# Retention attention feeding a leaky two-layer network: three more units transposed on TensorE, three more loaded through GpSimd's ring, zero matmuls in the opening, and layer-one blocks reordered

## The chip, the cores and the metric

The kernel runs on one core of one Trainium2 chip. A core has five engines that work at the same time and meet through semaphores: TensorE (PE in the profile: matmuls, and PEld its weight loads), VectorE (DVE), ScalarE (ACT), GpSimd (POOL) and SyncE (SP). SP, ACT and POOL also issue DMAs. The metric is the device time of one execution in microseconds (us); lower is better.

## The reference

```python
# q, k, v: batch 8, heads 8, sequence 576, head size 64 (float32)
scores = (q @ k^T) / 8
ret    = scores * Dmat         # Dmat[h, i, j] = gamma_h ** (i - j) for i >= j, else 0
x      = (ret @ v), heads side by side      # 4608 tokens x 512
h      = x @ w_in                           # 512 -> 2048
out    = max(0.01 * h, h) @ w_out           # 2048 -> 512, float32
```

There is no softmax, so the product with the decay can be done in chunks of 64 rows, with a running state (k^T v, 64x64 for each head) that carries what came before.

## The kernel before, in words

**Units.** Each batch's 576 rows are cut into four units of 128 rows and one of 64, 40 units in all. Units 4, 9, 14 and so on are the half ones. For a unit, `load` brings its q, k and v from HBM into tiles `t32` (one DMA each; six buffers for each of q, k and v). `cast_qk` writes 16-bit k (on ACT, L138) and q times a decay table (L139, on DVE for units under 8, on POOL from 8 on) into `qk16`; `cast_v` (L159) does the same for v. Both q and k are needed with the head dimension on the partitions, in `qkT`. For units under `NPE = 4` `transposes` does this on TensorE (eight 128x128 matmuls against an identity, L177, into the PSUM tile `yps`, copied out by ACT and DVE, L182). For all others `cast_qk` issues a transposing DMA from SP (L147).

**Attention of a unit.** `scores` (L194, L204) makes the chunk products and the state products in the PSUM tile `sc`, of which there is one buffer; `masks` (L214) and `states` (L228 to L242) read it on DVE, and ACT or POOL cast the state `st`. `outputs` (L296, L306; `outputs_acc`, L262 and L273, for the first four units) makes the unit's columns of `xT`, the 16-bit transposed input of the network: PE into `ot`, ACT copies (L314), DVE adds (L320).

**Network.** Tokens are cut into groups: three of 256, seven of 512, one of 256. A block of layer one (`g1_blocks`, L413) is eight matmuls of 256 columns or four of 512, followed by the leaky activation on ACT (L420) into `gt`. A block of layer two (`g2_blocks`, L436) is four matmuls of 512 columns; after sixteen of them DVE copies the result (L446) and SP stores it. `blocks(g, part, ...)` runs two blocks of layer one of group g for each part, sixteen matmuls. The layer two of groups 0 and 1 is done by `g2_wide` (L481): sixteen pieces of four matmuls, called in portions by `some(a, b)`, with four results in PSUM at once; DVE copies them (L490) and SP stores them (L492).

**Order.** The schedule is by hand: each engine runs its instructions in the order in which the program makes them. Lines 502 to 569 write out the opening, units 0 to 6 woven with groups 0 and 1. Units from 7 on are `steady(n)` steps: loads of unit n+4 (SP), scores of n, outputs of n-1, masks and states of n, casts of n+2 and with them its transposing DMA. `run` threads these steps between blocks of the network; the first such call holds the steps of units 7 to 11 among sixteen blocks of group 2.

**Loads.** Unit 0's k goes through SP. The rest of units 0 to 8, `w_in` (sixteen DMAs) and `w_out` (four) are issued by POOL and lie in one ring. Units 9 and 10 are issued by SP after the last piece of `g2_wide`, and units from 11 on by the steps. The transposing DMAs and the stores of results share SP's ring with SP's loads.

Of the kernel before, what the change touches and what calls it, by code (L numbers as in the profile page):

```python
# [9 lines left out]
FP = mybir.dt.float32  # L10
F16 = mybir.dt.float16
# [6 lines left out]
def kernel(  # L18
# [22 lines left out]
    nc = tc.nc  # L41
# [3 lines left out]
    P = 128  # L45
    CH = 64
    BLK = 256
    NP = H // 2
    NF = DFF // P
    TOK = 512  # L50
# [20 lines left out]
    const_pool = ctx.enter_context(tc.tile_pool(name="const", bufs=1))  # L71
# [4 lines left out]
    sc_pool = ctx.enter_context(tc.tile_pool(name="scp", bufs=1, space=PSUM))  # L76
    ot_pool = ctx.enter_context(tc.tile_pool(name="otp", bufs=1, space=PSUM))
    h_pool = ctx.enter_context(tc.tile_pool(name="hpp", bufs=2, space=PSUM))
    y_pool = ctx.enter_context(tc.tile_pool(name="yp", bufs=2, space=PSUM))
# [4 lines left out]
    ident = const_pool.tile([P, P], F16, name="ident")  # L84
# [11 lines left out]
    units = [(b, w) for b in range(B) for w in range((S + P - 1) // P)]  # L96
    NU = len(units)
    nrows = [min(P, S - P * w) for b, w in units]
    NPE = 4
    NFIRST = 7  # L100
    NEARLY = 8
    t32 = {}
    qk16 = {}
    v16 = {}
    qkT = {}
# [10 lines left out]
    def load(u, x, eng):  # L116
        b, w = units[u]
        n = nrows[u]
        t = ld_pool.tile([P, H, D], FP, name=f"t32_{x}")
        t32[u, x] = t  # L120
        eng.dma_start(  # L121
            out=t[0:n],
            in_=(q, k, v)[x][b, :, P * w : P * w + n, :].rearrange("h t d -> t h d"),
        )

    def loads(u, eng):
        for x in (1, 0, 2):
            load(u, x, eng)

    def cast_qk(u):  # L130

        if u >= NU:
# [5 lines left out]
        nc.scalar.copy(out=t[0:n, 1], in_=t32[u, 1][0:n])  # L138
        (nc.vector if u < NEARLY else nc.gpsimd).tensor_tensor(  # L139
            out=t[0:n, 0],  # L140
# [3 lines left out]
        )  # L144
        if u >= NPE:
            qkT[u] = a_pool.tile([P, 2, NP, P], F16, name="qkT")
# [5 lines left out]
    def cast_v(u):  # L152
        if u >= NU:
# [4 lines left out]
        v16[u] = t  # L158
        (nc.vector if u < NEARLY else nc.gpsimd).tensor_tensor(  # L159
            out=t[0:n],  # L160
# [5 lines left out]
    def casts(u):  # L166
        cast_qk(u)
        cast_v(u)

    def transposes(u):  # L170

        n = nrows[u]
        qkT[u] = a_pool.tile([P, 2, NP, P], F16, name="qkT")
        for x in (1, 0):
            tr = y_pool.tile([P, NP, P], F16, name="yps")
            for p in range(NP):
                nc.tensor.transpose(  # L177
                    tr[:, p, :],
                    qk16[u][:, x, 2 * p : 2 * p + 2, :].rearrange("t h d -> t (h d)"),
                    ident,  # L180
                )
            (nc.scalar.copy if x else nc.vector.tensor_copy)(out=qkT[u][:, x], in_=tr)  # L182

    sc_tiles = {}

    def scores(u):

        nb = nrows[u] // CH
        a = sc_pool.tile([P, 2, 2, NP, CH], FP, name="sc")
        sc_tiles[u] = a  # L190
        for p in range(NP):
            for g in range(2):
                for j in range(nb):
                    nc.tensor.matmul(  # L194
                        out=a[half(j), g, 0, p, :],
                        lhsT=qkT[u][half(g), 1, p, half(j)],
                        rhs=qkT[u][half(g), 0, p, half(j)],
                        start=True, stop=True, skip_group_check=True,
                    )
        if nb == 2:  # L200
            for p in range(NP):
                for j in range(2):
                    for g in range(2):
                        nc.tensor.matmul(  # L204
                            out=a[half(g), j, 1, p, :],
                            lhsT=qk16[u][half(j), 1, 2 * p + g, :],
                            rhs=v16[u][half(j), 2 * p + g, :],
                            start=True, stop=True, skip_group_check=True,
                        )

    def masks(u):
        n = nrows[u]
        s16s[u] = a_pool.tile([P, 2, NP, CH], F16, name="s16")
        nc.vector.tensor_tensor(  # L214
            out=s16s[u][0:n],
            in0=sc_tiles[u][0:n, :, 0],
            in1=mask_sb[0:n].unsqueeze(1).unsqueeze(1).to_broadcast([n, 2, NP, CH]),
            op=MUL,
        )

    def states(u):
        b, w = units[u]
        if nrows[u] < P:
            return
        st = sc_tiles[u][:, :, 1]
        s32 = a_pool.tile([P, 2, NP, CH], FP, name="s32")
        if w == 0:
            nc.vector.tensor_copy(out=s32[:, 0], in_=st[:, 0])  # L228
        else:
            nc.vector.tensor_tensor(out=s32[:, 0], in0=st[:, 0], in1=carry[b], op=ADD)  # L230
        if w % 2 == 0:
            nc.vector.tensor_tensor(out=s32[:, 1], in0=st[:, 1], in1=s32[:, 0], op=ADD)  # L232
        else:
            tmp = a_pool.tile([P, NP, CH], FP, name="stmp")
            nc.vector.tensor_tensor(out=tmp, in0=st[:, 1], in1=s32[:, 0], op=ADD)
            nc.vector.tensor_tensor(
                out=s32[:, 1], in0=tmp,
                in1=gblk_sb.unsqueeze(2).to_broadcast([P, NP, CH]), op=MUL,
            )
        carry[b] = s32[:, 1]  # L240
        st16[u] = a_pool.tile([P, 2, NP, CH], F16, name="st16")
        (nc.scalar.copy if u < NEARLY else nc.gpsimd.tensor_copy)(out=st16[u], in_=s32)  # L242

# [5 lines left out]
    def outputs_acc(u):  # L249

        n = nrows[u]
        b, w = units[u]
        ot = ot_pool.tile([P, 2, 2 * NP, CH], FP, name="ot")
        o_all = ot[:, 0].rearrange("q (p j) t -> q p j t", j=2)
        seen = set()
        for r in range(2):
            if r:
                nc.tensor.drain()
            for p in range(NP):
                for hh in range(2):  # L260
                    o = hh ^ swap(p)
                    nc.tensor.matmul(  # L262
                        out=o_all[half(o), p, r, :],
                        lhsT=v16[u][half(r), 2 * p + hh, :],
                        rhs=s16s[u][half(r), hh, p, :],
                        start=o not in seen, stop=False, skip_group_check=True,
                    )
                    seen.add(o)
            for j in range(2):
                if w == 0 and j == 0:  # L270
                    continue
                for p in (0, 2, 1, 3):
                    nc.tensor.matmul(  # L273
                        out=o_all[half(r ^ swap(p)), p, j, :],
                        lhsT=st_before(u, j)[half(r), p, :],
                        rhs=qkT[u][half(r), 0, p, half(j)],
                        start=False, stop=True, skip_group_check=True,
                    )
        t0 = (b * S + P * w) % XR
        nc.scalar.copy(  # L280
            out=xT[:, :, t0 : t0 + n], in_=o_all.rearrange("q p j t -> q p (j t)")
        )
# [62 lines left out]
    nc.vector.memset(warm, 0.0)  # L345
    nc.scalar.activation(out=warm, in_=warm, func=mybir.ActivationFunctionType.Lrelu)
    nc.vector.memset(zst, 0.0)

    load(0, 1, nc.sync)
    load(0, 0, nc.gpsimd)  # L350
# [10 lines left out]

    def steady(n):
        def go():
            if n + 4 < NU:
                loads(n + 4, nc.sync)
            if n < NU:
                scores(n)
            if n > NFIRST:
                outputs(n - 1)
            if n < NU:  # L370
                masks(n)
                states(n)
            casts(n + 2)

        steps.append((n - 1, go))
# [120 lines left out]
    def blocks(g, *parts):  # L496
        for fq in parts:
            for m in (2 * fq, 2 * fq + 1):
                g1[g][m]()
# [5 lines left out]
    cast_v(1)  # L505
    transposes(1)
    scores(0)
    masks(0)
    cast_qk(2)
    states(0)  # L510
    cast_v(2)
    for u in (2, 3):
        transposes(u)
        scores(u - 1)
        outputs_acc(u - 2)
        masks(u - 1)
        if u == 2:
            cast_qk(3)
        states(u - 1)
        if u == 2:  # L520
            cast_v(3)
# [4 lines left out]
    states(3)  # L526
    blocks(0, 1)
    outputs_acc(3)
    blocks(1, 0, 1)
    blocks(0, 2)  # L530
    blocks(1, 2)
    for u in (5, 6):
        loads(u, nc.gpsimd)
        load_w_out(u - 4)
    load_w_out(3)
    for u in (7, 8):
        loads(u, nc.gpsimd)
    casts(4)
    blocks(0, 3)
    casts(5)  # L540
    blocks(1, 3)

    wide = g2_wide([(0, 0), (0, 1), (1, 0), (1, 1)])
# [1 line left out]
    def some(a, b):  # L545
        for m in range(a, b):
            wide[m]()

    some(0, 3)
    scores(4)  # L550
    masks(4)
    some(3, 6)
    scores(5)
    outputs(4)
    masks(5)
    states(5)
    casts(6)
    some(6, 11)
    scores(6)
    outputs(5)  # L560
    masks(6)
    states(6)
    some(11, 13)
    outputs(6)
    some(13, 16)
    loads(9, nc.sync)
    casts(7)
    loads(10, nc.sync)
    casts(8)
    run(ends[3], g1[2] + g2_blocks(2))  # L570
    run(ends[4], g1_blocks(3))
# [33 lines left out]
```

## Time and profile before

| | |
|---|---|
| time, median of 3 runs | 352.72 us (351.57 to 354.4) |
| the profiled execution: its own time / its span | 352.5 us / 350.7 us |
| PE busy | 301.6 us, 86% of the span |
| DVE, ACT, POOL busy | 144.3, 134.4, 114.7 us |
| HBM read, written | 36.78 MB, 9.44 MB |
| POOL's ring (q0), SP's ring (q1) | 10.62 MB in 6400 packets, 39.73 MB in 126112 packets |

The span runs from the first to the last instruction; the execution's own time is 1.8 us more. In the page's slices each digit is the busy share of a fortieth of the span (8.77 us) in tenths. A timeline row reads: start, duration, engine, line, operation, output<-inputs, shapes, count; in brackets how long the engine stood idle just before and what released it. Rows of one kind that follow each other are merged and counted.

### The profile page before, as it was taken

Reading aid. Unit: us, or ns where it says so; the run is one execution under the profiler, and the core shown is the slowest. Engines: PE = TensorE matmul, PEld = TensorE weight load, DVE = VectorE, ACT = ScalarE, POOL = GpSimd, SP = SyncE. Lnnn points to the kernel's source line nnn. Section 1 sums busy time; section 2 is a strip of 40 time slices with the busy share of each in tenths; the row PEclk is TensorE's granted clock in tenths of the full one; section 3 lists DMA queues with packets and bytes.
Section 4 is the critical chain, followed back from the end, with each engine's and each line's share of the span. In section 5 each row is a group of like instructions: output and inputs, shape, how many; then the busy total and the mean of one; then the engine's idle time right before and its main releaser. Section 6 shows DMA issues by size and latency. Waiting matters only on the chain.

```text
span 350.7 us, 8376 instructions
## 1 busy us (share of the span) xinstructions
PE 301.6 (86%) x3544; PEld 155.8 (44%) x3544; DVE 144.3 (41%) x322; ACT 134.4 (38%) x237; POOL 114.7 (33%) x139
## 2 busy tenths in 40 slices
PE   1589955844849559999999999999999999999995
PEld 0367722323624224444444444444444444445552
DVE  2741202471536654633446256435634653200111
ACT  3345600132513456443454445445444534332220
POOL 8787612002442445252235043522252230000000
PEclk9999966896798999999999999999999999999999
DMA  8999994139999999996577889978977430010112
GB/s 181 211 202 173 225 219 93 31 130 211 187 167 168 199 219 167 183 188 157 123 170 172 176 129 195 208 169 169 169 174 145 109 59 32 31 60 32 60 39 82
DMA packets 132838, 50.97 MB, mean 145 GB/s; under 512 B 122528, under 2 KB 126624, under 8 KB 132800
## 3 DMA queue, kind: packets, MB, share of 16 engines
q1 hardware_dynamic: 126112, 39.73, 58.1%
q0 software_dynamic: 6400, 10.62, 16.1%
q8 instruction: 28, 0.46, 0.6%
q10 hardware_dynamic: 288, 0.08, 0.1%
q14 instruction: 10, 0.08, 0.1%
HBM read 36.78 MB, written 9.44 MB: 132 GB/s over the span
## 4 chain that ended last, share of the span: by engine, by line
PE 68%; DMA 13%; POOL 6%; issue 5%; DVE 3%; SPq 2%; ACT 1%; POOLq 0%; ACTq 0%
PE hps L413 32%; PE yps L436 30%; DMA qkT<-qk 10%; DMA t<-in_q_dram 3%; POOL t L121 2%; PE sc L194 2%; POOL qk L139 2%; POOL v L159 2%; SPq L121 1%; PE ot L306 1%; DVE xT L320 1%; PE ot L296 1%; PE sc L204 1%; SPq L147 1%; DVE osb L490 1%
## 5 line engine op out<-in xcount | busy, mean ns | idle before, releaser
L413 PE MATMUL hps<-xT,w_in 128*128 128x512 f16 (+1 forms) x704 | 150.4, 353 | 2.2 <-ACT xT L280 1.4
L420 ACT ACTIVATE gt<-hps 128x512 f16<-128x512 f32 x144 | 86.0, 597 | 124.2 <-PE hps L413 124.0
L436 PE MATMUL yps<-w_out,gt 128*128 128x512 f16 x512 | 129.6, 383 | 0.0
L413 PEld LDWEIGHTS <-w_in 128*128 128x128 f16 x704 | 69.9, 102 | 59.7 <-issue 2.9
L320 DVE TENSOR_TENSOR xT<-ot,own 64x256 f16<-64x256 f32 (+1 forms) x144 | 50.3, 388 | 91.2 <-ACT own L314 90.7
L436 PEld LDWEIGHTS <-gt 128*128 128x128 f16 x512 | 49.5, 99 | 57.7 <-issue 2.2
L242 POOL CAST st<-s 128x512 f16<-128x512 f32 x25 | 15.3, 610 | 129.9 <-DVE s L232 65.9
L446 DVE COPY osb<-yps 128x512 f32<-128x512 f32 x32 | 22.0, 688 | 71.1 <-PE yps L436 71.1
L139 POOL TENSOR_TENSOR qk<-t,cs 128x512 f16<-128x512 f32 (+1 forms) x32 | 33.3, 1042 | 32.7 <-DMA t<-in_q_dram 32.7
L314 ACT COPY own<-ot 128x512 f32<-128x512 f32 (+1 forms) x36 | 19.4, 538 | 53.6 <-PE ot L306 33.8
L194 PE MATMUL sc<-qkT 64*64 64x64 f16 x576 | 13.6, 207 | 28.9 <-DMA qkT<-qk 26.6
L214 DVE TENSOR_TENSOR s<-sc,cs 128x512 f16<-128x512 f32 (+1 forms) x40 | 27.6, 689 | 21.0 <-PE sc L194 10.0
L159 POOL TENSOR_TENSOR v<-t,cs 128x512 f16<-128x512 f32 (+1 forms) x32 | 33.3, 1042 | 0.6 <-PE ot L296 0.6
L194 PEld LDWEIGHTS <-qkT 64*64 64x64 f16 x576 | 9.0, 115 | 45.6 <-DMA qkT<-qk 31.6
L138 ACT CAST qk<-t 128x512 f16<-128x512 f32 (+1 forms) x40 | 24.7, 619 | 4.7 <-DMA t<-in_k_dram 4.7
L177 PE MATMUL yps<-ident,qk 128*128 128x128 f16 x32 | 4.7, 308 | 11.2 <-ACT qk L138 7.5
L306 PE MATMUL ot<-qkT,st 64*64 64x64 f16 x456 | 11.8, 197 | 1.6 <-ACT st L242 1.6
L296 PE MATMUL ot<-s,v 64*64 64x64 f16 x512 | 11.6, 196 | 1.2 <-DVE s L214 1.2
L139 DVE TENSOR_TENSOR qk<-t,cs 128x512 f16<-128x512 f32 (+1 forms) x8 | 5.5, 690 | 16.3 <-DMA t<-in_q_dram 14.8
L481 PEld LDWEIGHTS <-gt 128*128 128x128 f16 x64 | 7.1, 117 | 10.0 <-issue 6.0
L242 ACT CAST st<-s 128x512 f16<-128x512 f32 x7 | 4.3, 618 | 17.2 <-DVE s L232 12.0
L336 POOL DMA_DIRECT2D w_in<-in_moe_w_in_dram x16 | 9.5, 609 | 3.5 <-DMA t<-in_v_dram 1.6
(36 smaller groups left out, 147.6 us busy)
## 6 DMA issues: line engine op xcount, KB each, us to landing
out_dram<-osb SPq DMA_DIRECT2D x36, 256.0 KB, 2.3
t<-in_k_dram SPq DMA_DIRECT2D x25, 256.0 KB, 4.0
t<-in_q_dram SPq DMA_DIRECT2D x24, 256.0 KB, 4.5
t<-in_v_dram SPq DMA_DIRECT2D x24, 256.0 KB, 4.9
t<-in_q_dram POOLq DMA_DIRECT2D x8, 256.0 KB, 8.1
t<-in_v_dram POOLq DMA_DIRECT2D x8, 256.0 KB, 8.5
w_in<-in_moe_w_in_dram POOLq DMA_DIRECT2D x16, 128.0 KB, 4.9
w_out<-in_moe_w_out_dram POOLq DMA_DIRECT2D x4, 512.0 KB, 11.1
```

The lines of the kernel that those rows point to most:

```text
L138: nc.scalar.copy(out=t[0:n, 1], in_=t32[u, 1][0:n])
L139: (nc.vector if u < NEARLY else nc.gpsimd).tensor_tensor(out=t[0:n, 0], in0=t32[u, 0][0:n], in1=tab_sb[0:n, w % 2, 0, :].unsqueeze(2).to_b ...
L159: (nc.vector if u < NEARLY else nc.gpsimd).tensor_tensor(out=t[0:n], in0=t32[u, 2][0:n], in1=tab_sb[0:n, w % 2, 1, :].unsqueeze(2).to_broa ...
L194: nc.tensor.matmul(out=a[half(j), g, 0, p, :], lhsT=qkT[u][half(g), 1, p, half(j)], rhs=qkT[u][half(g), 0, p, half(j)], start=True, stop=T ...
L214: nc.vector.tensor_tensor(out=s16s[u][0:n], in0=sc_tiles[u][0:n, :, 0], in1=mask_sb[0:n].unsqueeze(1).unsqueeze(1).to_broadcast([n, 2, NP, ...
L242: (nc.scalar.copy if u < NEARLY else nc.gpsimd.tensor_copy)(out=st16[u], in_=s32)
L314: nc.scalar.copy(out=tmp[:, :, 0:nb, :], in_=own[:, 0:nb].rearrange("q j p t -> q p j t"))
L320: nc.vector.tensor_tensor(out=xT[half(o), ps, t0 : t0 + n].rearrange("q p (j t) -> q p j t", t=CH), in0=far[half(o), o ^ c, :, 0:nb, :], i ...
L413: nc.tensor.matmul(out=hps[:, f, :], lhsT=w_in16[:, c, fc * P : (fc + 1) * P], rhs=xT[:, c, t0 % XR : t0 % XR + tok], start=(c == 0), stop ...
L420: nc.scalar.activation(out=g_tiles[g][:, fb * nf : (fb + 1) * nf, :], in_=hps, func=mybir.ActivationFunctionType.Lrelu,)
L436: nc.tensor.matmul(out=y_cur[g, tb], lhsT=g_tiles[g][:, f, tb * P : (tb + 1) * P], rhs=w_out16[:, f, :], start=(f == 0), stop=(f == NF - 1),)
L446: nc.vector.tensor_copy(out=osb, in_=y_cur[g, tb])
```

## The change

Units 4, 5 and 6 are transposed on TensorE too. Units 4 and 5 use the `yps` buffers; unit 6 uses one tile in the pool of `sc`. The transposes handle only the unit's own rows. Units 9, 10 and 11 are issued by POOL, behind unit 8. Four matmuls on a tile of zeros stand after `scores(0)`, and three each in the two turns of the loop over units 2 and 3. Blocks of layer one of groups 0 and 1 come in another order, with the casts, transposes and scores of units 4 and 5 among them, and the portions of `g2_wide` are cut anew; the casts of unit 7 stand before its last three pieces.

```diff
-    NPE = 4
+    NPE = 7
     NFIRST = 7
     NEARLY = 8
+    NRING = 11
-    def transposes(u):
+    def transposes(u, pool=None):
         n = nrows[u]
         qkT[u] = a_pool.tile([P, 2, NP, P], F16, name="qkT")
+        if pool is None:
+            trs = [y_pool.tile([P, NP, P], F16, name="yps") for x in range(2)]
+        else:
+            both = pool.tile([P, 2, 2 * NP, P], F16, name="sc")
+            trs = [both[:, x, 0:NP, :] for x in range(2)]
         for x in (1, 0):
-            tr = y_pool.tile([P, NP, P], F16, name="yps")
             for p in range(NP):
                 nc.tensor.transpose(
-                    tr[:, p, :],
-                    qk16[u][:, x, 2 * p : 2 * p + 2, :].rearrange("t h d -> t (h d)"),
-                    ident,
+                    trs[x][:, p, 0:n],
+                    qk16[u][0:n, x, 2 * p : 2 * p + 2, :].rearrange("t h d -> t (h d)"),
+                    ident[0:n, 0:n],
                 )
-            (nc.scalar.copy if x else nc.vector.tensor_copy)(out=qkT[u][:, x], in_=tr)
+            (nc.scalar.copy if x else nc.vector.tensor_copy)(
+                out=qkT[u][:, x, :, 0:n], in_=trs[x][:, :, 0:n]
+            )
...
+    idle = const_pool.tile([P, TOK], F16, name="idle")
+    nc.vector.memset(idle, 0.0)
+    def keep_warm(n):
+        t = h_pool.tile([P, 1, TOK], FP, name="hps")
+        for _ in range(n):
+            nc.tensor.matmul(out=t[:, 0, :], lhsT=idle[:, 0:P], rhs=idle, start=True, stop=True)
...
     def steady(n):
         def go():
-            if n + 4 < NU:
+            if NRING < n + 4 < NU:
                 loads(n + 4, nc.sync)
...
     scores(0)
+    keep_warm(4)
     masks(0)
...
         outputs_acc(u - 2)
+        keep_warm(3)
         masks(u - 1)
...
     outputs_acc(3)
-    blocks(1, 0, 1)
     blocks(0, 2)
-    blocks(1, 2)
+    blocks(1, 0)
...
-    for u in (7, 8):
+    for u in (7, 8, 9, 10, 11):
         loads(u, nc.gpsimd)
     casts(4)
+    blocks(1, 1)
+    transposes(4)
+    blocks(1, 2)
+    scores(4)
+    casts(5)
+    masks(4)
     blocks(0, 3)
-    casts(5)
+    transposes(5)
     blocks(1, 3)
...
-    some(0, 3)
-    scores(4)
-    masks(4)
-    some(3, 6)
+    some(0, 2)
     scores(5)
     outputs(4)
     masks(5)
     states(5)
+    some(2, 4)
     casts(6)
-    some(6, 11)
+    some(4, 6)
+    transposes(6, sc_pool)
+    some(6, 8)
     scores(6)
     outputs(5)
     masks(6)
     states(6)
+    some(8, 11)
+    outputs(6)
     some(11, 13)
-    outputs(6)
+    casts(7)
     some(13, 16)
-    loads(9, nc.sync)
-    casts(7)
-    loads(10, nc.sync)
     casts(8)
```

## The prediction

> **What bounds the kernel now.** I read the page's slices first, to see when each resource is full, then sums by stage.
>
> ```profile
> PE   1589955844849559999999999999999999999995
> ...
> DMA  8999994139999999996577889978977430010112
> ```
> ```profile
> 0.00:20.90 20.90, 8.63 (x185) 6.23 (x186) 11.41 (x24) 8.50 (x15) 16.71 (x27) 1.00 0.99 197
> 20.90:41.80 20.90, 20.04 (x224) 15.94 (x224) 4.62 (x8) 12.02 (x21) 15.35 (x21) 1.00 1.15 199
> 41.80:75.80 34.00, 21.95 (x219) 9.30 (x217) 11.12 (x26) 4.96 (x10) 5.32 (x6) 0.80 0.55 109
> 75.80:133.00 57.20, 36.91 (x671) 20.96 (x671) 26.99 (x63) 20.71 (x38) 21.27 (x24) 0.88 1.13 196
> 133.00:320.00 187.00, 187.00 (x2095) 88.16 (x2093) 85.98 (x196) 83.44 (x148) 56.05 (x64) 1.00 0.70 138
> ```
>
> A row gives the stretch, its length, then busy time of PE, PEld, DVE, ACT and POOL, the granted clock, the DMA share and GB/s. From 133 us on PE has no gap (187.00 of 187.00) and DMA is at 0.70. So whatever brings PE to that point earlier is kept to the end, one for one. Before it PE stands idle 12.3, 0.9, 12.1 and 20.3 us in the four stretches. In the third DMA is largely idle too (share 0.55; slices 7 and 8 show 4 and 1 tenths): there the change can work. The rows of PE show what it waits for and how fast it runs.
>
> ```profile
> 20.86 3.57 PE L413 MATMUL hps<-xT,w_in 128*128 128x256 f16 x16 [0.68 <-ACT xT L280]
> 26.08 3.60 PE L413 MATMUL hps<-xT,w_in 128*128 128x256 f16 x16
> 30.33 0.30 PE L273 MATMUL ot<-qkT,st 64*64 64x64 f16 x8
> 31.30 10.73 PE L413 MATMUL hps<-xT,w_in 128*128 128x256 f16 x96 [0.68 <-ACT xT L280]
> 41.87 1.89 PE L481 MATMUL yps<-w_out,gt 128*128 128x512 f16 x8
> 43.60 1.03 PE L481 MATMUL hps<-w_out,gt 128*128 128x512 f16 x4
> 48.53 0.42 PE L194 MATMUL sc<-qkT 64*64 64x64 f16 x8 [3.91 <-DMA qkT<-qk]
> 58.10 0.43 PE L194 MATMUL sc<-qkT 64*64 64x64 f16 x16 [4.10 <-DMA qkT<-qk]
> 58.98 3.60 PE L481 MATMUL hps<-w_out,gt 128*128 128x512 f16 x8
> 66.35 0.32 PE L194 MATMUL sc<-qkT 64*64 64x64 f16 x16 [0.46 <-DMA qkT<-qk]
> 72.00 0.25 PE L306 MATMUL ot<-qkT,st 64*64 64x64 f16 x8 [1.57 <-ACT st L242]
> 82.65 0.43 PE L194 MATMUL sc<-qkT 64*64 64x64 f16 x16 [5.79 <-DMA qkT<-qk]
> 83.23 3.60 PE L413 MATMUL hps<-xT,w_in 128*128 128x256 f16 x16
> 87.50 0.43 PE L194 MATMUL sc<-qkT 64*64 64x64 f16 x16 [0.67 <-DMA qkT<-qk]
> 104.21 0.32 PE L194 MATMUL sc<-qkT 64*64 64x64 f16 x16 [2.97 <-DMA qkT<-qk]
> ```
>
> Scores of units 4, 5, 6, 7 and 8 begin at 48.53, 58.10, 66.35, 82.65 and 87.50, each behind a transposing DMA; 104.21 is unit 11. Sixteen matmuls of 256 columns take 3.57 to 3.60 us when the clock is low and 10.73/6 = 1.79 us when it is high; eight of 512 take 1.73 us high (41.87 to 43.60), 3.4 us low (58.98 to 62.37). So the waits of 4 us cost twice: themselves, and slow matmuls behind them.
>
> The transposing DMAs explain the waits:
>
> ```profile
> 41.36 16.69 DMA qkT<-qk
> ...
> 63.26 3.04 DMA qkT<-qk
> ```
> ```profile
> 45.12 0.88 POOL L121 DMA_DIRECT2D t<-in_v_dram  x1 [0.41 <-issue]
> ```
> ```profile
> q0 software_dynamic: 1046, 2.13, 76.2%
> q1 hardware_dynamic: 1498, 0.37, 20.0%
> ...
> t<-in_v_dram POOLq DMA_DIRECT2D x1, 256.0 KB, 12.6
> ```
>
> Unit 5's, issued at 41.36, took 16.69 us; unit 6's took 3.04. The difference is POOL's ring: its last load (unit 8's v) is issued at 45.12 and lands 12.6 us later, at 57.7, and unit 5's transpose lands with it, at 58.05. The last fence is the DMA traffic from 45 to 58 us: 2.13 MB of loads through q0, while the transposes (q1) took 20.0% of the engines.
>
> **The change, part by part.**
>
> *Zero matmuls in the opening: 0 us.* At the low clock each costs about 2 x 0.22 = 0.44 us (the 3.4 us row, per matmul). The four after `scores(0)` and the first three lie in gaps: PE works only 8.63 of the first 20.90 us, because it waits for loads and casts. The last three (1.3 us) begin at about 20.2 and fill a 0.68 us wait: cost at most 0.6 us. If they raise the clock for the two stretches at 20.86 and 26.08, the gain is at most 2 x (3.6 - 1.8) = 3.6 us; but units 4 and 5 come from the ring at fixed times:
>
> ```profile
> 34.35 0.68 DVE L139 TENSOR_TENSOR qk<-t,cs 64x512 f16<-64x512 f32 x1 [7.36 <-DMA t<-in_q_dram]
> 37.41 0.69 DVE L139 TENSOR_TENSOR qk<-t,cs 128x512 f16<-128x512 f32 x1 [1.55 <-ACT gt L420]
> ```
>
> Without any gain PE reaches `transposes(4)` at 30.63 + 3 x 1.79 = 36.0 (three `blocks` parts; the 0.68 us wait at 31.30 goes, as group 0's part needs no new xT). Unit 4's q is cast at 35.03. So only 1 us of an early start can be used. Bounds -1 to +0.6; I take 0.
>
> *Units 4 to 6 on TensorE.* Eight transposes of the opening are one row, and the casts and copies that a unit passes through are others:
>
> ```profile
> 17.20 1.03 PE L177 MATMUL yps<-ident,qk 128*128 128x128 f16 x8 [1.20 <-DVE qk L139]
> ...
> 18.99 0.58 ACT L182 COPY qkT<-yps 128x512 f16<-128x512 f16 x1
> ```
> ```profile
> 62.62 0.61 ACT L138 CAST qk<-t 128x512 f16<-128x512 f32 x1
> 71.33 0.62 ACT L242 CAST st<-s 128x512 f16<-128x512 f32 x1 [3.60 <-DVE s L236]
> ```
> ```profile
> 72.93 1.53 DVE L320 TENSOR_TENSOR xT<-ot,own 64x256 f16<-64x256 f32 x4 [1.08 <-ACT own L314]
> 74.49 0.69 DVE L490 COPY osb<-yps 128x512 f32<-128x512 f32 x1
> ```
>
> 1.03 us at the low clock; 0.7 is my estimate at the high one. The copies of units 4 and 5 (0.58 on ACT) lie beside `blocks(1, 2)` and `blocks(1, 3)`, 1.79 us each; unit 6's beside `some(6, 8)`, 1.73. Without that cover each would cost its 0.6 us. The walk of PE:
>
> - 30.63 + 10.73 (the same 96 layer-one matmuls) + 2 x 0.7 + 0.42 (scores of 4) = 43.2: start of `g2_wide`, with no DMA wait behind it.
> - `some(0, 2)`, 1.73: scores of 5 at 44.9 (before: 58.10). From there to unit 6's k cast the order of ACT and DVE is as before: 58.10 to 63.23, 5.13 us, so 50.0. PE has only 0.9 + 3.46 us of work for it and waits under 1 us.
> - Transposes of 6 to 50.7, `some(6, 8)` to 52.4: scores of 6 at 52.4 (66.35). From there to the state cast 66.35 to 71.95, 5.60 us: 58.0. PE has 0.64 + 2.6 us of cover (three pieces, before two), and waits about 2.4; that chain was there before.
> - Then `outputs(6)`; its xT adds are done 72.00 to 74.46 = 2.46 us later, 60.5; one result copy, 0.69, and unit 7's q cast, 0.69: 61.9. **Unit 7's transposing DMA is issued at 61.9** (before: 79.12).
>
> *Units 9 to 11 through POOL's ring.* POOL's queue gets nine more issues, and only unit 8's casts stand behind them. What it does to unit 7's transpose is the disputed term.
>
> ```profile
> 79.12 1.26 SPq L147 DMA_TRANSPOSE qkT<-qk  x1
> ```
>
> Undisturbed: 79.12 to 82.65 = 3.5 us, so scores of 7 at 65.4. Beside a busy ring: 9.5 us (48.53, when unit 4's landed, to 58.05), so 71.4; counted from its issue, 16.69, so 78.6. When is the ring empty? Without the transposes of 4 and 5, which took 20.0% of 13 us, it is through with unit 8 at 57.7 - 2.6 = 55.1. Unit 9 is half: 0.39 MB; 10 and 11 have 0.79 MB each; 1.97 MB at 2.13 MB in 10.1 us (45.0 to 55.1), 0.21 MB/us, take 9.3 us: 64.4. So the transpose runs 2.5 us beside the ring (2.5/9.5 = 26% of it) and the other 74% alone (2.6 us): **scores of 7 at 67.0**. I take that, nearest to both rows; ends 65.4 and 78.6.
>
> The Trainium skill, "DMA: Bandwidth & Descriptors", section "SWDGE vs HWDGE vs iDMA", says that GpSimd's DMAs and the hardware-issued ones sit in different queues inside each DMA engine, which serves its queues in turn. That speaks against this part of the change: loads pulled forward through the ring slow every transpose of SP beside them. The trace agrees (16.69 us beside the ring, 3.04 without). By the rule unit 7's would not be undisturbed, and scores of 7 would come 1.6 us later than at 65.4, as by the row; with no sharing the forecast would be 1.6 us lower.
>
> *Unit 8 and what follows.* SP holds three stores before unit 8's transpose. Their copies end at 61.9 + 0.69 + 3 x 0.69 = 64.7, so it is issued at about 66 and follows unit 7's by the usual 3 us: **scores of 8 at 70.0**, against 87.50. PE, having two blocks (1.8 us) between them, is not the later one. From scores of 8 to scores of 11 it is 104.21 - 87.50 = 16.7 us in a chain of ACT, DVE, POOL and transposes over two steps; step 9 on issues the same loads and transposes in the same order, and SP's loads begin earlier. I keep that distance, and the rest to 133 us. The 1.97 MB moved from the full stretch (DMA share 1.13) to the empty one could quicken it; the bound is unit 9's transpose, which now has no load of unit 11 ahead of it, at most 2 us. I count none.
>
> **Sum.** 87.5 - 70.0 = 17.5 us earlier, PE without a gap behind it: 352.5 (the profiled execution) - 17.5 = **335.0 us**. Its time lies 0.2 us under the median shown, so 335 stands for the median too. This is well outside 1%, which is about what a measurement of this kernel can tell from no change.
>
> **Rivals.**
>
> - *Clock kept up (faster than I say).* If no gap of PE is long, the slow stretches go: 3.60 against 1.79 at 83.23, and the loss before units 12 on. Against: 16.7 us from 8 to 11 hold some 10 us of PE work, so gaps return. With scores of 7 at 65.4 and 8 at 69, 18.5 us, and one slow stretch less, 1.8 us: 332 us.
> - *Unit 7 starves.* The ring serves the transpose 9.5 us, whatever is left in it: scores of 7 at 71.4, of 8 at 71.4 + 4.3 (83.18 to 87.50 by the rows of unit 8's issue and scores) = 75.7: 11.8 us gained, 340.7 us. For: 9.5 us is measured. Against: 2.5 us of ring work remain at its issue.
>
> ```profile
> 83.18 1.99 SPq L147 DMA_TRANSPOSE qkT<-qk  x1
> ```
>
> - *Nothing moves.* The scores of 4 to 6 come early, but the steps behind are set by something not seen here, such as DMA throughput (196 GB/s at share 1.13 in that stretch): within 3 us of 352. Against: 1.97 MB of that stretch's traffic move into a stretch at 109 GB/s.
> - *Slower.* One mechanism: the deeper ring keeps the transposes of 7, 8 and 9 slow throughout. 61.9 + 16.69 = 78.6 for 7, then 9.5 for 8: 88.1, and 8.9 (39.61 to 48.53, unit 4's, half) for 9: 97.0 against 93.74, +3.3 us: 356. It turns slower from the point where the ring still holds loads at 88 us, that is if 1.97 MB took 33 us instead of 9.3.
>
> ```profile
> 39.61 1.29 SPq L147 DMA_TRANSPOSE qkT<-qk  x1
> ...
> 93.74 0.25 PE L194 MATMUL sc<-qkT 64*64 64x64 f16 x4 [1.15 <-DMA qkT<-qk]
> ```
>
> **How the numbers follow.** Forecast (331 to 339) 0.60; clock kept up 0.14; unit 7 starves (338 to 346) 0.18; nothing moves 0.05; slower 0.03. The range from 329 to 344 holds the first two and most of the third, some 0.85 of the chance; a tail of slips in the walk is why I do not narrow it. Faster by over 1% are the first three, 0.92; within 1% 0.05; slower 0.03.
>
> **What would show it.** Scores of 4, 5 and 6 with no DMA in front, at about 38, 45 and 52; last ring load landing near 64; scores of 7 near 67 and of 8 near 70; 16.7 us from 8 to 11; PE without gaps from about 115 on. Wrong if the clock falls inside `g2_wide` (then its 64 matmuls take up to 14 us more), if unit 7 waits past 72, or if the distance from 8 to 11 changes by over 3 us.

## The result, and the profile after

The changed kernel takes 338.82 us (338.4 to 339.79, 4 runs) against 353.56 us for the kernel before on the same chip; the ratio is 0.959, 95% interval 0.954 to 0.965. In a later group it took 336.44 us against 353.42 (0.954, 0.950 to 0.958), so one version differs by some 2 us from group to group, and smaller differences are read from traces, not times. The profiled execution has a span of 337.3 us (350.7 before). Two of the six executions of `cast7_early` below, the profiled one among them, one of six of `add_last` and one of ten of `dma_456` were in a slower state, so the times given leave these out, and of the trace of `cast7_early` only single instructions are used.

The first view is the sums by stage of the changed kernel, cut where its work stands as in the prediction's table (columns as there).

```profile
20.90:43.10 22.20, 19.24 (x250) 15.41 (x249) 5.95 (x12) 12.71 (x23) 16.79 (x23) 0.92 1.13 205
43.10:66.70 23.60, 16.87 (x218) 7.91 (x216) 14.55 (x28) 5.51 (x10) 13.59 (x16) 1.00 1.01 201
66.70:124.20 57.50, 42.44 (x696) 22.98 (x699) 28.96 (x69) 24.34 (x44) 22.29 (x25) 0.88 1.09 180
124.20:306.50 182.30, 182.30 (x2075) 86.39 (x2075) 82.63 (x188) 79.84 (x141) 53.01 (x60) 1.00 0.64 136
```

The third stretch of before (34.0 us, DMA at 0.55, 12.1 us of idle PE) has become one of 23.6 us with DMA at 1.01 and 6.7 us of idle PE. From 124.2 us on PE has no gap and runs at full clock, as before from 133 on. The second view is PE's timeline of the changed kernel; lines have moved, L201 is the former L194 and L428 the former L413.

```profile
20.86 1.91 PE L428 MATMUL hps<-xT,w_in 128*128 128x256 f16 x16
...
34.29 0.29 PE L182 MATMUL yps<-ident,qk 64*128 64x64 f16 x4 [1.99 <-ACT qk L139]
...
35.46 3.00 PE L428 MATMUL hps<-xT,w_in 128*128 128x256 f16 x16
38.39 0.42 PE L201 MATMUL sc<-qkT 64*64 64x64 f16 x8
...
44.88 0.32 PE L201 MATMUL sc<-qkT 64*64 64x64 f16 x16
...
52.93 0.32 PE L201 MATMUL sc<-qkT 64*64 64x64 f16 x16
...
66.72 1.77 PE L428 MATMUL hps<-xT,w_in 128*128 128x256 f16 x8 [3.45 <-DVE osb L505]
68.42 0.43 PE L201 MATMUL sc<-qkT 64*64 64x64 f16 x16
...
72.08 0.32 PE L201 MATMUL sc<-qkT 64*64 64x64 f16 x16 [0.57 <-DMA qkT<-qk]
...
87.59 0.32 PE L201 MATMUL sc<-qkT 64*64 64x64 f16 x16 [2.11 <-DMA qkT<-qk]
...
115.38 0.43 PE L201 MATMUL sc<-qkT 64*64 64x64 f16 x16 [2.99 <-DMA qkT<-qk]
...
116.38 7.85 PE L428 MATMUL hps<-xT,w_in 128*128 128x512 f16 x24
124.16 0.32 PE L201 MATMUL sc<-qkT 64*64 64x64 f16 x16
```

Scores of units 4, 5 and 6 stand at 38.39, 44.88 and 52.93 with no DMA in their brackets. Scores of 7, 8, 11 and 17 are at 68.42, 72.08, 87.59 and 124.16: 14.2, 15.4, 16.6 and 13.7 us earlier than before (unit 17 was at 137.86 then, the last line of the next fence, which is of the kernel before). The gain grows to unit 11 and shrinks by 2.9 us up to 17.

```profile
132.46 5.47 PE L413 MATMUL hps<-xT,w_in 128*128 128x512 f16 x24
137.86 0.32 PE L194 MATMUL sc<-qkT 64*64 64x64 f16 x16
```

The wait of 3.45 us before unit 7 is not one that the prediction named. PE's block needs a PSUM buffer that DVE has to copy out. The next fences are the timelines of DVE, POOL and SP at that place, in the changed kernel.

```profile
61.08 0.69 DVE L505 COPY osb<-yps 128x512 f32<-128x512 f32 x1
61.80 3.06 DVE L140 TENSOR_TENSOR qk<-t,cs 128x512 f16<-128x512 f32 x1
64.78 0.68 DVE L160 TENSOR_TENSOR v<-t,cs 128x512 f16<-128x512 f32 x1
```
```profile
59.30 0.88 POOL L122 DMA_DIRECT2D t<-in_v_dram  x1
60.27 1.05 POOL L140 TENSOR_TENSOR qk<-t,cs 128x512 f16<-128x512 f32 x1
61.27 1.04 POOL L160 TENSOR_TENSOR v<-t,cs 128x512 f16<-128x512 f32 x1
62.27 1.03 POOL L140 TENSOR_TENSOR qk<-t,cs 64x512 f16<-64x512 f32 x1
63.27 1.03 POOL L160 TENSOR_TENSOR v<-t,cs 64x512 f16<-64x512 f32 x1
```
```profile
64.96 1.33 SPq L148 DMA_TRANSPOSE qkT<-qk  x1
```

DVE's q cast of unit 7 reads two tensors from SBUF. It takes 0.68 to 0.69 us elsewhere, and here 3.06: it ends at 64.86, just after POOL's row of four casts (64.30). The first two of the four are unit 8's and came at 57.4 and 59.0 us before, while DVE made no cast; now they stand behind POOL's last load issue at 59.30. The other two are unit 9's. They came at 81.3 and 82.3 us before, and follow at once now, as unit 9's data come through the ring. So all four lie in DVE's way. Everything behind the cast waits: the result copies (PE's 3.45 us) and unit 7's transposing DMA, issued at 64.96.

### The profile page after: what moved, and what is told of

It is laid out like the page before. It is cut to its first block, busy times and chain, and to the rows that moved or that the text cites. A ratio compares the mean times of both kernels' runs of the same rounds, so it can differ in the third digit from the quotient of the medians.

```text
span 337.3 us, 8449 instructions
## 1 busy us (share of the span) xinstructions
PE 299.5 (89%) x3578; PEld 154.7 (46%) x3578; DVE 147.8 (44%) x326; ACT 135.6 (40%) x240; POOL 122.0 (36%) x148
## 4 chain that ended last, share of the span: by engine, by line
PE 65%; DMA 13%; issue 10%; POOL 9%; SPq 1%; DVE 0%; POOLq 0%
PE yps L451 31%; PE hps L428 29%; DMA t<-in_v_dram 6%; DMA w_out<-in_moe_w_out_dram 5%; POOL t L122 3%; POOL v L160 2%; POOL qk L140 2%; DMA qkT<-qk 2%; PE sc L201 2%; POOL w_in L343 2%; PE ot L313 1%; PE ot L303 1%; PE sc L211 1%; SPq L122 1%; SPq L148 0%
## 5 line engine op out<-in xcount | busy, mean ns | idle before, releaser
L428 PE MATMUL hps<-xT,w_in 128*128 128x512 f16 (+1 forms) x704 | 151.2, 352 | 3.6 <-DVE osb L505 3.4
L451 PE MATMUL yps<-w_out,gt 128*128 128x512 f16 x512 | 127.9, 379 | 0.0
L428 PEld LDWEIGHTS <-w_in 128*128 128x128 f16 x704 | 68.8, 101 | 62.7 <-issue 9.6
L451 PEld LDWEIGHTS <-gt 128*128 128x128 f16 x512 | 49.1, 98 | 56.4
L201 PE MATMUL sc<-qkT 64*64 64x64 f16 x576 | 13.5, 205 | 14.6 <-DMA qkT<-qk 11.2
L201 PEld LDWEIGHTS <-qkT 64*64 64x64 f16 x576 | 9.0, 113 | 30.5 <-DMA qkT<-qk 17.2
L182 PE MATMUL yps<-ident,qk 128*128 128x128 f16 (+1 forms) x48 | 5.9, 274 | 11.3 <-ACT qk L139 8.4
L140 DVE TENSOR_TENSOR qk<-t,cs 128x512 f16<-128x512 f32 (+1 forms) x8 | 7.9, 986 | 18.0 <-DMA t<-in_q_dram 18.0
L122 POOL DMA_DIRECT2D t<-in_q_dram x12 | 10.5, 877 | 3.8 <-DVE qk L140 1.9
L122 POOL DMA_DIRECT2D t<-in_v_dram x12 | 10.2, 851 | 4.3 <-DMA t<-in_k_dram 1.5
L182 PEld LDWEIGHTS <-qk 128*128 128x128 f16 (+1 forms) x56 | 4.4, 119 | 16.1 <-ACT qk L139 11.1
```

The lines of the kernel that those rows point to most:

```text
L122: eng.dma_start(out=t[0:n], in_=(q, k, v)[x][b, :, P * w : P * w + n, :].rearrange("h t d -> t h d"),)
L140: (nc.vector if u < NEARLY else nc.gpsimd).tensor_tensor(out=t[0:n, 0], in0=t32[u, 0][0:n], in1=tab_sb[0:n, w % 2, 0, :].unsqueeze(2).to_b ...
L201: nc.tensor.matmul(out=a[half(j), g, 0, p, :], lhsT=qkT[u][half(g), 1, p, half(j)], rhs=qkT[u][half(g), 0, p, half(j)], start=True, stop=T ...
L428: nc.tensor.matmul(out=hps[:, f, :], lhsT=w_in16[:, c, fc * P : (fc + 1) * P], rhs=xT[:, c, t0 % XR : t0 % XR + tok], start=(c == 0), stop ...
L451: nc.tensor.matmul(out=y_cur[g, tb], lhsT=g_tiles[g][:, f, tb * P : (tb + 1) * P], rhs=w_out16[:, f, :], start=(f == 0), stop=(f == NF - 1),)
```

## The experiments

**The zero matmuls** (`no_zero`).

```diff
-    keep_warm(4)
...
-        keep_warm(3)
```

> The changed kernel without its ten zero matmuls. Theory A (the gain comes from the waits on the transposing DMAs of units 4 to 6, which are gone): the first two stretches of sixteen layer-one matmuls take 3.6 us again instead of 1.9, but the end of layer one of groups 0 and 1 stays within 1 us, because in the changed kernel PE waited 2.0 and 0.7 us for unit 4's casts; time 338 to 340. Rival B (the clock in the opening is the gain): the 4 us by which the opening came earlier are lost, 342 to 343.

Measured: 337.68 us (336.23 to 338.74), ratio 0.956 (0.952 to 0.961): no slower than with them. PE's timeline, and DVE's one row:

```profile
21.90 3.15 PE L428 MATMUL hps<-xT,w_in 128*128 128x256 f16 x14 [0.37 <-DMA w_in<-in_moe_w_in_dram]
...
34.61 0.29 PE L182 MATMUL yps<-ident,qk 64*128 64x64 f16 x4 [0.16 <-ACT qk L139]
...
43.46 0.32 PE L201 MATMUL sc<-qkT 64*64 64x64 f16 x16
```
```profile
60.38 4.32 DVE L140 TENSOR_TENSOR qk<-t,cs 128x512 f16<-128x512 f32 x1
```

The first stretch of sixteen takes 1.91 us with the zeros, and here 3.15 for fourteen; the second, which was said to be slow again too, takes 1.92 in both. That the zeros raise the clock is inferred from these durations alone: the profile's clock column reads 1.00 at this place in both runs, and in the control below, with the zeros, the first stretch takes 2.97 (granted 0.62). But PE meets unit 4's casts at the same time, 34.3 or 34.6; with the zeros it waits 1.99 us there, and its next sixteen matmuls run at the low clock (3.00 us at 35.46; granted 0.61). Rival B, the clock, falls. Unit 5 even comes 1.4 us earlier here, and that is lost again in the cast, 4.32 us, which ends at 64.70 (64.86 with the zeros): scores of 7 are at 68.34.

**Units 4 to 6 back on the transposing DMA** (`dma_456`).

```diff
-    NPE = 7
+    NPE = 4
...
-    transposes(4)
...
-    transposes(5)
...
-    transposes(6, sc_pool)
```

> The changed kernel with units 4, 5 and 6 transposed by SP's DMA again, loads and order as changed. Theory A: their transposes run beside a ring that stays busy until about 66 us; scores of 4 near 45, of 5 past 56, of 6 near 68, of 7 near 82; time 350 to 356, the whole gain gone. Rival C (the early loads of units 9 to 11 are the gain): scores of 7 later by the waits of units 4 to 6, but the steps behind run faster, 342 to 347.

Measured: 353.25 us, ratio 1.000 (0.997 to 1.004). The whole gain is gone. The chain and PE's timeline show why:

```profile
39.83 17.78 DMA qkT<-qk
62.82 9.00 DMA qkT<-qk
```
```profile
71.86 0.43 PE L201 MATMUL sc<-qkT 64*64 64x64 f16 x16 [5.80 <-DMA qkT<-qk]
...
84.94 0.32 PE L201 MATMUL sc<-qkT 64*64 64x64 f16 x16 [0.30 <-DMA qkT<-qk]
```

Unit 5's transpose takes 17.78 us beside the ring; unit 6's, 3.04 before, now 9.00, since the ring is busy longer. Scores of 6 and 7 come 5.5 and 2.3 us later than before; by unit 11 (104.55 against 104.21) nearly all of that is made up. So the longer ring, the zeros and the new order without the transposes on TensorE are no help. The order of the blocks was not taken back by itself.

**Units 9 to 11 back on SP** (`loads_sp`).

```diff
-            if NRING < n + 4 < NU:
+            if n + 4 < NU:
...
-    for u in (7, 8, 9, 10, 11):
+    for u in (7, 8):
...
     some(13, 16)
+    loads(9, nc.sync)
+    loads(10, nc.sync)
     casts(8)
```

> The changed kernel with units 9, 10 and 11 loaded by SP at the places they had before. Theory A: POOL's casts of unit 8 come at about 55 instead of 60.3, unit 7's q cast on DVE takes 0.7 us instead of 3.06, scores of 7 near 66; the loads then stand ahead of unit 8's transpose, and scores of 8 to 11 keep the distances they had before the change (4.9 and 16.7 us): scores of 11 near 88, time 338 to 341. Rival C (early loads are the gain): at least 5 us slower than the changed kernel, 344 or more.

Measured: 341.45 us (338.54 to 343.19), ratio 0.965 (0.959 to 0.971). That lies between the two theories. The interval overlaps that of the changed kernel's first group (0.954 to 0.965) and lies just above that of the later one (0.950 to 0.958): by the ratios the ring is worth some 2 or 4 us, so the time does not settle it. The trace shows the mechanism (SP, then PE):

```profile
73.31 2.36 SPq L148 DMA_TRANSPOSE qkT<-qk  x1
```
```profile
68.37 0.32 PE L201 MATMUL sc<-qkT 64*64 64x64 f16 x16 [0.40 <-DMA qkT<-qk]
77.96 0.43 PE L201 MATMUL sc<-qkT 64*64 64x64 f16 x16 [7.29 <-DMA qkT<-qk]
```

POOL's casts of unit 8 come at 55.97 and 56.98 here, and DVE's q cast of unit 7, at 64.39, is short (0.69 us). Yet scores of 7 are no earlier, as this execution came to unit 6 later (54.82). Six loads stand on SP ahead of unit 8's transpose, and PE waits 7.29 us for it (0.57 with the ring). Between units 7 and 8 that costs 5.9 us more, where Theory A had kept the old distance.

**Casts of units 8 and 9 on DVE** (`dve_casts`).

```diff
-        (nc.vector if u < NEARLY else nc.gpsimd).tensor_tensor(   # in cast_qk and cast_v
+        (nc.vector if u < 10 else nc.gpsimd).tensor_tensor(
```

> The changed kernel with the q and v casts of units 8 and 9 on DVE instead of POOL. If POOL's casts from 60.3 to 64.3 us are what stretched unit 7's q cast on DVE to 3.06 us, it takes 0.7 us here, the wait of 3.45 us for the result copies falls to about 1, and scores of 7 come 1.5 to 2.5 us earlier (66 to 67); time 336 to 338. If the cast was long because unit 7's data were late, it stays near 3 us and the time near 338.8. If the busy ring slows unit 7's transpose as predicted, PE then waits for it (68.4 again) although the cast is short.

Measured: 336.91 us (336.28 to 338.22), ratio 0.954 (0.949 to 0.958), which overlaps the changed kernel's.

```profile
62.98 0.69 DVE L140 TENSOR_TENSOR qk<-t,cs 128x512 f16<-128x512 f32 x1
```
```profile
65.52 1.03 PE L428 MATMUL hps<-xT,w_in 128*128 128x256 f16 x8 [0.30 <-DVE osb L505]
68.23 0.32 PE L201 MATMUL sc<-qkT 64*64 64x64 f16 x16 [1.67 <-DMA qkT<-qk]
```

With POOL silent the cast takes 0.69 us and the wait of 3.45 us shrinks to 0.30: with the short cast of `loads_sp` the collision is shown. But scores of 7 stay at 68.23, because a DMA wait of 1.67 us takes the place; the third outcome of the expectation.

**Unit 7's casts earlier, and casts ahead of the states in the steps** (`cast7_early`, `cast_first_only`, `cast_first`, with the changed kernel as control).

```diff
     states(6)
+    casts(7)              # cast7_early, cast_first
     some(8, 11)
...
     some(11, 13)
-    casts(7)
...
+            casts(n + 2)   # cast_first_only, cast_first
             if n < NU:
                 masks(n)
                 states(n)
-            casts(n + 2)
```

> The changed kernel again, as the control of this group. 338 to 340; unit 7's q cast on DVE is again stretched to 3 us or more until POOL's casts of units 8 and 9 end.

> The changed kernel with the casts of unit 7 placed right behind states(6), so that DVE makes them near 58 us, before POOL begins its casts of unit 8 at 60.3, and SP issues unit 7's transposing DMA near 59.3 instead of 65.0, while POOL's ring is busy until about 66. If the busy ring slows the transpose as I predicted (9.5 us beside it), it lands near 67 and PE waits about 2 us for it; scores of 7 at 67, time 336.5 to 338. If the ring hardly slows it, scores of 7 come as soon as the result copies free the buffer, at 65.5, and the time is 335 to 336.5. If the stretched cast did not matter, 338.8 as before.

> The changed kernel with casts(n+2) ahead of masks and states in the steps, so that POOL no longer holds the q cast of unit n+2 behind the state cast of unit n. If the pace of the steps from unit 8 to 17 (5.3 to 5.8 us each) is the chain DVE states, POOL state cast, POOL q cast, transposing DMA, the waits on those DMAs (2.2, 2.1, 2.8, 0.6, 3.0 us) go and the wait on the one score tile (4.7 us a step) is next: 8 to 17 in 43 to 46 us instead of 52, time 331 to 335. If the pace is set by DMA throughput (196 to 207 GB/s in that stretch), it stays at 5.2 us or so and the time at 337 to 339.

> Both moves together: casts of unit 7 behind states(6), and casts ahead of masks and states in the steps. If the two are independent, the gains add: 2 us and 4 to 7 us, 329 to 333. If DMA throughput sets the pace of the steps, 336 to 338.

| | us | ratio to before, 95% |
|---|---|---|
| control | 336.44 | 0.954 (0.950 to 0.958) |
| cast7_early | 337.75 | 0.954 (0.950 to 0.959) |
| cast_first_only | 334.68 | 0.946 (0.942 to 0.950) |
| cast_first | 332.66 | 0.941 (0.939 to 0.944) |

The control came out faster than the 338 to 340 expected; its q cast of unit 7 is stretched again, to 3.67 us. `cast7_early` gains nothing over it. In its trace the opening ran later, and the collision only moved to the v cast of unit 7 (DVE):

```profile
61.04 5.40 DVE L160 TENSOR_TENSOR v<-t,cs 128x512 f16<-128x512 f32 x1
```

In `cast_first` the early cast got through (0.69 us), so its trace measures the term that the prediction disputed, undisturbed by the collision: the DMA issued at 59.2 us, beside the ring, and PE behind it.

```profile
qkT<-qk SPq DMA_TRANSPOSE x1, 9.9
```
```profile
69.19 0.43 PE L201 MATMUL sc<-qkT 64*64 64x64 f16 x16 [4.81 <-DMA qkT<-qk]
73.29 0.43 PE L201 MATMUL sc<-qkT 64*64 64x64 f16 x16
...
118.38 0.32 PE L201 MATMUL sc<-qkT 64*64 64x64 f16 x16
```

It lands 9.9 us after its issue, with the ring's last load (issued at 59.78, landing 9.4 us later). Issued at 61.8 (`cast7_early`) it took 6.6 us, at 63.8 (`dve_casts`) 4.4 and at 65.0 (the changed kernel) 3.1: an earlier issue is eaten up by the ring, and it lands at 68 to 69 in all four. The gain of `cast_first` is in the steps: units 8 to 17 take 45.1 us, against 52.1 in the changed kernel's first profile, 49.1 in the control's (70.83 to 119.91) and 47.2 in that of `cast_first_only` (43 to 46 were expected there). Here are PE's waits from 72 to 125 us, of the changed kernel's first profile, of the control and of `cast_first`; a line reads: total, number, longest.

```profile
PE sc L201 <- DMA qkT<-qk: 11.2, 6, 3.0
PE sc L201 <- DVE s L239: 2.1, 1, 2.1
```
```profile
PE sc L201 <- DMA qkT<-qk: 6.8, 5, 2.1
```
```profile
PE sc L201 <- DMA qkT<-qk: 2.9, 1, 2.9
PE sc L201 <- DVE s L239: 2.6, 2, 2.1
PE sc L201 <- DVE s L221: 2.5, 2, 1.3
```

POOL's q cast no longer waits for the state cast of two units earlier (unit 10's comes at 64.76 instead of the first profile's 77.76), so the DMA starts earlier. Its wait falls to 2.9 us, from 6.8 in the control of the same group (11.2 in the first profile); it is 5.0 in `cast_first_only`. Waits for the one score tile come up in its place.

**What is left** (`pe7`, `add_last`, `pe7_add_last`). `pe7` is `cast_first` with unit 7 on TensorE too; in `add_last` DVE makes the xT adds after masks and states.

```diff
-    NPE = 7
+    NPE = 8                                # pe7
...
-    some(11, 13)
-    some(13, 16)
-    casts(8)
+    some(11, 12)
+    transposes(7, sc_pool)
+    casts(8)
+    some(12, 16)
...
-                outputs(n - 1)
+            finish = outputs(n - 1, later=True)   # add_last: all but the four adds
             casts(n + 2); masks(n); states(n)     # shortened
+            finish()
```

> cast_first, and unit 7 is transposed on TensorE too (in the score tile, behind outputs(6)), with the casts of unit 8 ahead of the last four pieces of the wide layer two. In cast_first unit 7's DMA transpose was issued at 59.2 and landed 9.9 us later beside POOL's ring, PE waited 4.8 us. If that wait is a real bound, scores of 7 come at about 65 and of 8 at about 69 (unit 8's transpose now runs beside the end of the ring), time 328 to 331. If unit 8's transpose, or the steps behind it, only take over the wait, 331 to 333 as in cast_first.

> cast_first, and in the steps DVE makes masks and states of unit n ahead of the xT adds of unit n-1. In cast_first PE's waits in the steps were on DVE's reads of the one score tile (1.2, 0.4, 2.1, 1.3 us) and one DMA wait of 2.9. If the score tile sets the pace there, 1.5 us a step go: scores of 8 to 17 in 40 to 42 us instead of 45, 328 to 330. If DMA throughput is already the pace (193 GB/s at share 1.17), DMA waits replace them: 331 to 333.

> Both. If both bounds are real, 325 to 328; if DMA throughput is what is left, 328 to 331.

Measured: 332.66 us, 0.943 (0.939 to 0.946); 335.10, 0.948 (0.945 to 0.951); 332.15, 0.941 (0.938 to 0.944). None beats `cast_first`. In `pe7` unit 7 comes at 67.94, 1.3 us earlier, and not at 65. PE does not wait in the 7 us ahead of it; the sixteen matmuls of the last four pieces, behind the transposes, run at a low clock (granted 0.56 from 60.87 to 66.98; eight take 1.89 us at full clock):

```profile
60.87 3.62 PE L496 MATMUL yps<-w_out,gt 128*128 128x512 f16 x8
64.28 2.85 PE L496 MATMUL hps<-w_out,gt 128*128 128x512 f16 x8
```

Unit 8 is then 3.1 us earlier than in `cast_first` (70.17), but of that only 1.3 is left at unit 17 (117.10). In `add_last` PE's waits in the steps are

```profile
PE sc L201 <- DMA qkT<-qk: 9.1, 6, 3.2
```

so the score tile's waits are gone and DMA waits are back, as in its second outcome, at 197 GB/s and a share of 1.16 (193 and 1.17 in `cast_first`). That DMA throughput sets the pace is argued, not shown. The time is above the 331 to 333 of that outcome, and the trace shows one more reason: the early v cast of unit 7 (DVE) met POOL's row after all.

```profile
59.64 7.07 DVE L160 TENSOR_TENSOR v<-t,cs 128x512 f16<-128x512 f32 x1
```

So unit 8 starts 1.8 us later than in `cast_first` (75.13), and the comparison of the two mixes this with the moved adds, behind which units 8 to 17 take 47.1 us instead of 45.1. In `pe7_add_last` the same cast takes 7.22 us; its time is above both of its forecasts. `cast_first`, `pe7` and `pe7_add_last` are the fastest of all, and the interval of each lies below both of the changed kernel's.

## Why the prediction was right, point by point

The forecast was 335.0 us, 17.5 us less than the profiled execution; the first group gave 14.7 us less by the medians, the second 17.0.

- **The walk to unit 6 held**: 38, 45 and 52 were said, 38.39, 44.88 and 52.93 came (36.29, 42.31 and 50.35 in the control). `dma_456` shows that the transposes on TensorE are necessary for the gain: without them all of it goes.
- **Zero matmuls at nothing held** (`no_zero`), for the reason given: unit 4's data come at a fixed time. The low clock that the prediction reads off the first stretches is an inference: the clock column reads 1.00 there, and 0.50 at the later slow rows (58.98 and 83.23).
- **Unit 7 at 67.0 was 68.42, by another path.** The step that failed is "one result copy, 0.69, and unit 7's q cast, 0.69: 61.9": the cast took 3.06. Its root is the sentence that "only unit 8's casts stand behind" POOL's nine new issues. I asked what waits for them on POOL, and not what they collide with on DVE when they come later; and unit 9's casts stand behind too. The Trainium skill, "SBUF — State Buffer", section "Who interferes with whom", says that a DVE instruction with two SBUF inputs contends with a GpSimd instruction that reads SBUF. The trace agrees (0.69 us against 3.06 to 7.22).
- **The ring was to be through at 64.4**; its last load landed at 66.4 (issued at 59.30, 7.1 us on its way). The price of the transpose, 9.5 us beside the ring, is right (9.9 and 9.0 measured). With 61.9 for the issue and 66.4 for the ring the prediction's own rule gives 4.5 us beside it and 1.8 alone, so 68.2; `cast7_early`, issued at 61.8, took 6.6. In the first profile the transpose was issued 3.1 us late, at 65.0, and so ran nearly alone (3.1 us). That the late cast and the late ring end within 1.4 us of 67.0 is partly luck; in the control unit 7 came at 66.73.
- **Unit 8 at 70.0 was 72.08**: 1.4 us from unit 7, and 3.7 us between them instead of 3.0.
- **16.7 us from 8 to 11 were 15.5**, within the 2 us that I left uncounted.
- **The rest lost 2.9 us in the first profile**, where I had counted none: 24 matmuls at 116.38 took 7.85 us at the low clock (granted 0.67), behind a DMA wait of 2.99, against 5.47 for the same 24 before. PE has no gap from 115.4 on, as was said, but a stretch without gaps is not one at full clock. The control's profile shows no such stretch (5.47 us), and there unit 17 stands at 119.91, 18.0 us earlier than before. So this part differs between executions of the same kernel, and no one walk can give it.

Of the rivals, "unit 7 starves" has its price right, but the transpose takes that long only with an early issue, as in `cast_first` (59.2), and then lands no later than the ring's last load. "Clock kept up" did not come: eight matmuls took 1.77 us at 66.72, with a granted clock of 0.54. "Nothing moves" and "slower" are refuted by the time. What stays open is the worth of the ring in time (2 or 4 us, with intervals that overlap in one group) and that of the new order of the blocks by itself.

## What to carry to other kernels

Where a transposing DMA shares the engines with a deep ring of loads, count its landing from the end of the ring (in four runs here 68 to 69 us, whether it was issued at 59 or at 65), or move that transpose to an engine that has slack. When an engine's work is put behind longer queues, ask not only who waits for it, but what it will now run beside. A cast moved out of the way only just in time can be caught again in another version: the early casts got through in `cast_first` and `pe7`, and not in `add_last`. Raising the clock ahead of a wait for data buys only what the data's time leaves.

## What the runs showed of the hardware that was not expected

A DVE cast of two SBUF inputs is held by a whole row of POOL casts, not by one: 3.06, 4.32 and 5.40 us instead of 0.69 beside rows of four casts of about 1 us, 4.02, 7.07 and 7.22 beside rows of six (`cast_first_only`, `add_last`, `pe7_add_last`). In all six it ends some 0.6 us after the row's last cast. The casts of 5.40, 7.07 and 7.22 us are recorded as started 0.5 to 0.8 us before the row's first; why these did not get through first stays open. POOL's own casts keep their 1.03 to 1.06 us. POOL's load issues do not do this: a DVE cast beside one (58.51 in `cast_first`, the issue at 58.64) took 0.68 us.
